# One large change to the gate, FFN and FFT-mixer training step: tail position, chain order, sigmoids, dB scaling and drain copies

## The chip, the cores and the metric

The kernel runs on one core of one Trainium2 chip. The metric is the device time of one execution in microseconds (us). Each of the kernel's executions is given, and their median is the kernel's time. A profiled execution also has a span (first to last recorded instruction) and a trace of every instruction.

## The reference

With S = 2048 tokens, D = 576 columns, F = 4608 hidden columns, all in bf16:

```python
g = sigmoid((x * gate_w).sum(-1, keepdims=True))
a = irfft2(rfft2(x) * (w_r + 1j * w_i))              # over tokens and columns
b = (gelu(x @ w_gate) * (x @ w_up)) @ w_down         # tanh form of gelu
out = g * a + (1 - g) * b
# returned: out, and for the given grad_out the gradients of
# x, w_r, w_i, w_gate, w_up, w_down, gate_w
```

The kernel names used below: dO is grad_out, dB = (1 - g) dO is the gradient that reaches b (held in SBUF, 128 tokens to a tile, 16 tiles), z = dO w_down^T, da = (1 - g) z, A the hidden activation gelu(gate)·up, dHg and dHu the gradients of the gate and up products. The gradient of w_down is A^T dB, those of w_gate and w_up are x^T dHg and x^T dHu.

## The kernel before

**Phase 1** loops over 18 column groups of F (g, FG = 256 columns each) and inside it over 4 token blocks (m, 4 tiles of 128 tokens). These 72 steps are numbered pr = 4 g + m from 0. A step does this:

- `H_mm` (lines 395 to 420) issues on TensorE: 16 full 128-row matmuls for z (line 402); whatever is handed in as `between`; the 4 row-tiled matmuls of z for the last 64 of the 576 contraction rows (line 407); and 4 row-tiled ones (64 rows) for xy, the gate and up products (line 411). `xy_full(0)` and `xy_full(1)` then issue the 8 + 8 full matmuls of xy (line 418). z has one PSUM buffer (its tag is shared with the transform's `pf`), xy has two.
- On ScalarE, `H_da` copies z into da, scaled, four instructions (line 430), and `H_act` evicts xy: q is the square of the gate product (line 437), xb the gate product (439), hu the up product (440).
- On VectorE, `H_ew1` (445 to 447) makes s, the argument of the tanh, and a polynomial in q. `H_ew2`, called `sigs()` in the loop, comes at the end of the step: ScalarE makes two sigmoids of s (lines 461, 462) and VectorE works a **chain** of eight operations (466 to 473) to A, dHu and dHg. A store (line 477, SP's queue) writes the three to DRAM for phase 2.
- da, xb and hu have two buffers each; q, s and om have one. dH comes from a ring (`keep`).

Between these stands other work for TensorE. **Weight-gradient units** of the group before (`W_units`) are split over the steps: `u_dwd` (line 509, 16 matmuls A·dB to a unit), `u_dw` (line 527, 16 matmuls x·dH), and one `tail` (line 541, 32 column-tiled matmuls for the last 64 columns of x). The tail is the `inside` job of step m = 2: it is handed to `H_mm` as `between`, so it lies between z's full and row-tiled matmuls, except in step 5, where it comes after `H_mm`. The units' PSUM results are copied out by `wevac` (line 486), on ScalarE, and on VectorE in step 6 after the point `run_late`. What is left of a group's units (`carry`, pend[4]) goes into the next group's first step. **Transform units** of the FFT branch (lines 570 to 850) are spread over the steps by a share of work, all through the one `pf` buffer, and evicted by ScalarE or VectorE. From about 370 to 630 us VectorE also has the products with w_r and w_i.

Group 0 is different: its steps 0 to 3 also transpose x and dO on TensorE (line 367) with copies on VectorE or ScalarE (line 374), compute the gate (line 383), and hold the chain back: the chain of step m runs in step m + 1 (`held`). Ahead of a held chain VectorE scales four tiles of dB in place (`scale_dB`, line 955), in steps 1 to 4. Step 5 builds two tables XR on VectorE (`build_R`, line 164); step 6 builds the B table (lines 225 to 239), whose last product (line 239) waits for a sine that ScalarE makes in `run_late`, between two loads of its function tables.

**Drain**: when the loop is over, the units of group 17 remain. The tail comes first, then `carry` (the last unit of group 16), then pend[0] to pend[4] (d0; d1 to d3; w0; w1 and w2; w3).

**Phase 2** (line 1168 on, matmuls of 128x288) makes b and the gradient of x from what was stored, fed by transposing loads (`pin`, six buffers, SP's queue).

## Time and profile before

| | us |
|---|---|
| median of 6 executions | 1413.31 |
| lowest, highest | 1412.71, 1415.09 |
| the profiled execution | 1414.85 |
| its span | 1413.1 |
| TensorE (PE) busy | 1378.0 |
| VectorE (DVE) busy | 734.1 |
| ScalarE (ACT) busy | 730.2 |
| GpSimd (POOL) busy | 244.6 |
| phase 2's first matmul (line 1168) at | 985.39 |
| mean granted TensorE clock | 0.996 |

How to read the views. A line of the timeline gives the start, the length and the engine of a run of equal instructions, the line of the kernel, the tile written and the tiles read with their shapes, the number of instructions, and in brackets how long the engine was idle before and who ended that ("<-DVE hu L472" is VectorE's instruction on line 472). A line of the windows gives a stretch, its length, the busy time and count of each engine (PE, the weight loads PEld, DVE, ACT, POOL), the granted TensorE clock (1.00 is full speed), the busy share of the DMA engines and GB/s. In the page's row PEclk each digit is the clock of a fortieth of the span in tenths, where 9 is 90% or more. Some matmul records are missing from the trace, so that a short idle time of PE with the releaser "issue" can be a lost record.

### The profile page before, as it was taken

The numbers are of one execution on the slowest core, as the hardware profiler recorded it, in microseconds if no ns is written. First come the engines' busy times: TensorE is split into PE (matmuls) and PEld (weight loads), VectorE is DVE, ScalarE is ACT, GpSimd is POOL, SyncE is SP. The second block draws the span as 40 slices with busy tenths as digits, with TensorE's granted clock in tenths as the row PEclk, the third lists the DMA queues.
The fourth block names the chain that finished last, engine by engine and source line by source line (L and its number), as shares of the span: only waits on it lengthen the run. The fifth ranks groups of instructions, "written<-read, shape, count | busy, mean of one in ns | idle before, by whom it ended". The sixth has DMA issues, their size and how long they took to land.

```text
span 1413.1 us, 25803 instructions
## 1 busy us (share of the span) xinstructions
PE 1378.0 (98%) x10181; PEld 915.1 (65%) x10272; DVE 734.1 (52%) x1400; ACT 730.2 (52%) x1325; POOL 244.6 (17%) x486
## 2 busy tenths in 40 slices
PE   8899999999999999999999999999999999999999
PEld 6456566565565556556566566555777777777777
DVE  7866565655788777885565656551000642212101
ACT  6777776777787878777777776671000000000000
POOL 3010101113353633423101111110000100000000
PEclk9999999999999999999999999999999999999999
DMA  6334344445455665556456464759999998777773
GB/s 206 101 87 133 94 135 120 108 118 164 119 132 152 159 164 147 134 150 164 127 142 169 128 170 134 182 122 263 191 187 202 223 193 166 166 158 163 158 151 90
DMA packets 510645, 214.48 MB, mean 152 GB/s; under 512 B 312538, under 2 KB 503708, under 8 KB 510524
## 3 DMA queue, kind: packets, MB, share of 16 engines
q1 hardware_dynamic: 493402, 187.44, 56.8%
q0 software_dynamic: 14912, 24.24, 6.1%
q8 instruction: 80, 1.31, 0.4%
q10 hardware_dynamic: 2210, 1.15, 0.3%
q14 instruction: 41, 0.34, 0.1%
HBM read 41.05 MB, written 93.84 MB: 95 GB/s over the span
## 4 chain that ended last, share of the span: by engine, by line
PE 87%; ACT 4%; issue 1%; DVE 1%; DVEq 0%
PE acc L1168 30%; PE wps L527 15%; PE xy L418 15%; PE wps L509 9%; PE z L402 8%; PE wps L541 2%; PE xy L411 2%; PE pf L570 2%; PE z L407 1%; PE pf L841 1%; ACT xb L439 1%; ACT q L437 1%; PE pf L768 1%; PE pf L843 1%; ACT hu L440 1%
## 5 line engine op out<-in xcount | busy, mean ns | idle before, releaser
L1168 PEld LDWEIGHTS <-pin 128*128 128x128 bf16 x3456 | 338.0, 98 | 85.8 <-issue 0.3
L527 PE MATMUL wps<-dH,xn 128*128 128x512 bf16 x1122 | 270.3, 381 | 4.4 <-DVE dwd L486 2.6
L418 PE MATMUL xy<-wgu,xT 128*128 128x512 bf16 x1091 | 259.8, 381 | 8.4 <-issue 7.6
L418 PEld LDWEIGHTS <-xT 128*128 128x128 bf16 x1152 | 106.9, 98 | 138.1 <-issue 31.0
L527 PEld LDWEIGHTS <-xn 128*128 128x128 bf16 x1152 | 111.8, 98 | 122.1 <-issue 5.8
L1185 ACT COPY bo<-acc 128x288 f32<-128x288 f32 x32 | 12.7, 398 | 305.0 <-PE acc L1168 280.4
L466 DVE TENSOR_TENSOR xb<-xb,s 128x1024 bf16<-128x1024 bf16 x72 | 49.8, 692 | 203.4 <-ACT s L462 203.3
L509 PE MATMUL wps<-dB,A 128*128 128x288 bf16 x1152 | 153.6, 286 | 0.0
L534 POOL DMA_DIRECT2D out_dram<-dw x134 | 72.8, 546 | 458.1 <-ACT dw L486 432.4
L1168 PE MATMUL acc<-wgT,pin 128*128 128x288 bf16 x1152 | 143.8, 286 | 0.0
L1168 PE MATMUL acc<-wuT,pin 128*128 128x288 bf16 x1152 | 143.6, 286 | 0.0
L1168 PE MATMUL acc<-wd_all,pin 128*128 128x288 bf16 x1152 | 142.6, 286 | 0.0
L402 PE MATMUL z<-wdT,dOT 128*128 128x256 bf16 x1152 | 138.1, 273 | 2.9 <-ACT Xg L684 1.0
L509 PEld LDWEIGHTS <-A 128*128 128x128 bf16 x1152 | 112.2, 98 | 33.1
L402 PEld LDWEIGHTS <-dOT 128*128 128x128 bf16 x1152 | 112.8, 98 | 26.7 <-issue 6.3
L430 ACT ACTIVATE da<-z,omg 128x256 bf16<-128x256 f32 x288 | 112.0, 470 | 9.0 <-PE z L407 4.9
L1240 DVE SCALAR_TENSOR_TENSOR f32t<-gwf,dlog,b16t 128x576 f32<-128x576 f32 x16 | 13.1, 818 | 175.5 <-DMA b16t<-dxa_scr 175.5
L439 ACT CAST xb<-xy 128x512 bf16<-128x512 f32 x144 | 85.1, 591 | 31.3 <-PE xy L418 31.3
L437 ACT ACTIVATE q<-xy 128x512 bf16<-128x512 f32 x144 | 88.1, 613 | 7.4 <-PE xy L418 5.3
L440 ACT CAST hu<-xy 128x512 bf16<-128x512 f32 x144 | 87.4, 607 | 0.0
L461 ACT ACTIVATE om<-s 128x1024 bf16<-128x1024 bf16 x72 | 76.3, 1060 | 5.8 <-DVE s L446 5.8
L486 ACT CAST dw<-wps 128x512 bf16<-128x512 f32 x72 | 42.1, 586 | 70.4 <-PE wps L527 66.8
(207 smaller groups left out, 1585.0 us busy)
## 6 DMA issues: line engine op xcount, KB each, us to landing
scr<-dH SPq DMA_DIRECT2D x144, 256.0 KB, 3.4
scr<-A SPq DMA_DIRECT2D x72, 256.0 KB, 2.5
out_dram<-dw POOLq DMA_DIRECT2D x134, 64.0 KB, 2.3
wd_all<-in_B_w_down_dram SPq DMA_DIRECT2D x3, 1728.0 KB, 8.2
out_dram<-dwd POOLq DMA_DIRECT2D x34, 144.0 KB, 3.3
scr_p<-Vt SPq DMA_DIRECT2D x32, 145.0 KB, 2.8
wgu<-in_B_w_gate_dram SPq DMA_DIRECT2D x18, 256.0 KB, 3.9
wgu<-in_B_w_up_dram SPq DMA_DIRECT2D x18, 256.0 KB, 3.4
```

Source lines behind the costliest of these rows:

```text
L402: nc.tensor.matmul(zo(t), lhsT=dOT[:, ci, t, :], rhs=wdT[:, ci, :], start=(t % 4 < 2 and ci == 0), stop=False)
L418: nc.tensor.matmul(xy[k][:, t % 2, :], lhsT=xT[:, ci, t, :], rhs=wgu[:, ci, :], start=False, stop=(ci == 3))
L430: nc.scalar.activation(da[:, t, :], z[:, t % 2, t // 2, :], ACT.Copy, scale=omg32[:, 4 * m + t:4 * m + t + 1])
L437: nc.scalar.activation(q[:, h, :], xy[:, :, 0:FG], ACT.Square)
L439: nc.scalar.copy(xb[:, h, :], xy[:, :, 0:FG])
L440: nc.scalar.copy(hu[:, h, :], xy[:, :, FG:2 * FG])
L461: nc.scalar.activation(om[:], s[:], ACT.Sigmoid, scale=-2.0 * C_GELU)
L466: V.tensor_tensor(xb[:], xb[:], s[:], op=ALU.mult)
L509: nc.tensor.matmul(wps[:, :288], lhsT=tl(0, t)[:, fch * P:(fch + 1) * P], rhs=dB[:, t, h * 288:(h + 1) * 288], start=(t == 0), stop=(t == ...
L527: nc.tensor.matmul(wps[:].rearrange("p a b -> p (a b)"), lhsT=xn[:, t, c * P:(c + 1) * P], rhs=kt[t // 4][1][:, t % 4].rearrange("p k f -> ...
L534: wst[0].dma_start(ov[:, c, fsl], dw[:, k, :])
L1168: nc.tensor.matmul(acc[:, :288], lhsT=src[:, r, :], rhs=w_of(r)[:, h * 288:(h + 1) * 288], start=(first and r == 0), stop=(last and r == F ...
```

## The change

Eight edits:

1. The `inside` job (the tail) comes after `H_mm` and `H_da` in every step, so between the row-tiled matmuls of xy and `xy_full(0)`.
2. dH is taken from its ring in `H_ew1`, where da·hu is written into dHg; in the chain dHu = da·xb comes second. The chain's last product is then made in place in dHg.
3. In groups 0 and 1 and in every step m = 2 only one sigmoid is made; 1 - s is made on VectorE into xb's buffer. In the other steps both sigmoids are made, the one that the chain needs first; the tag `om` becomes `sg`.
4. dB is scaled in steps 4 (tiles 0 to 3, ScalarE), 5 (4 to 7 ScalarE, 8 to 11 VectorE) and 6 (12 to 15, VectorE). Group 0's weight units are ordered anew: w2 in step 5, all four dwd units in step 6, w3 later.
5. The first copy of a transposed x tile goes to ScalarE in steps 1 and 2.
6. `build_R` for later tables adds a constant to the table before it, in place of four multiply-adds.
7. The B table's last product is issued after the step's other jobs and stores.
8. In the drain `carry` and d0 to d3 come ahead of the tail, and the copies of the dw results use the buffers of xb, hu and da in turn. The stores are ordered A, dHu, dHg.

```diff
--- before.py
+++ after.py
@@ -160,8 +160,15 @@
     n = 4
     step = 2.0 * math.pi / S * EPS_SCALE
     X = unit([n, P], I32, name="XR")
-    for t in range(n):
-        V.scalar_tensor_tensor(X[:, t, :], tb.kk[:, 0, :], tb.scol[:, t0 + t:t0 + t + 1], tb.kk[:, 1, :], op0=ALU.mult, op1=ALU.add)
+    if t0 == 0:
+        for t in range(n):
+            V.scalar_tensor_tensor(X[:, t, :], tb.kk[:, 0, :], tb.scol[:, t0 + t:t0 + t + 1], tb.kk[:, 1, :], op0=ALU.mult, op1=ALU.add)
+    else:
+        if t0 == n:
+            tb.k4 = unit([P], I32, name="k4")
+            V.tensor_scalar(tb.k4[:], tb.kk[:, 0, :], float(n), None, op0=ALU.mult)
+        V.tensor_tensor(X[:], tb.XR[:], tb.k4[:].unsqueeze(1).to_broadcast([P, n, P]), op=ALU.add)
+    tb.XR = X
     V.tensor_single_scalar(X[:], X[:], S - 1, op=ALU.bitwise_and)
     if t0 % 8 == 0:
         tb.Rpair = unit([8, P], name="Rt")
@@ -236,8 +243,12 @@
 
     def sines():
         nc.scalar.activation(o[:], Xi[:].rearrange("p v a b c d -> p v (a b c d)"), ACT.Sin, bias=tb.pi[:], scale=-step)
+
+    def signed():
         V.tensor_tensor(tb.B[:], o[:], ms[:].rearrange("p v a b c d -> p v (a b c d)"), op=ALU.mult)
     tb.late.append(sines)
+    yield
+    signed()
     yield
 
 
@@ -420,7 +431,7 @@
         return z, full
 
     def ewt(tag, g):
-        if tag in ("q", "s", "om"):
+        if tag in ("q", "s", "sg"):
             return unit([4, FG], name=tag) if g == 0 else ew.tile([P, 4, FG], BF16, tag=tag, name=tag, bufs=1)
         return ew.tile([P, 4, FG], BF16, tag=tag, name=tag, bufs=2)
 
@@ -439,13 +450,15 @@
             nc.scalar.copy(xb[:, h, :], xy[:, :, 0:FG])
             nc.scalar.copy(hu[:, h, :], xy[:, :, FG:2 * FG])
 
-    def H_ew1(g, tiles):
+    def H_ew1(g, tiles, da):
         xb, q, hu = tiles
         s = ewt("s", g)
         V.tensor_scalar(s[:], q[:], A_GELU, 1.0, op0=ALU.mult, op1=ALU.add)
         V.tensor_tensor(s[:], xb[:], s[:], op=ALU.mult)
         V.tensor_scalar(q[:], q[:], 6.0 * A_GELU * C_GELU, 2.0 * C_GELU, op0=ALU.mult, op1=ALU.add)
-        return s
+        dH = keep.tile([P, 4, 2, FG], BF16, tag="dH", name="dH")
+        V.tensor_tensor(dH[:, :, 0, :], da[:], hu[:], op=ALU.mult)
+        return s, dH
 
     stores = []
 
@@ -455,25 +468,30 @@
             stores.pop(0)()
             n -= 1
 
-    def H_ew2(g, m, tiles, s, da):
+    def H_ew2(g, m, tiles, s, dH, da):
         xb, q, hu = tiles
-        om = ewt("om", g)
-        nc.scalar.activation(om[:], s[:], ACT.Sigmoid, scale=-2.0 * C_GELU)
-        nc.scalar.activation(s[:], s[:], ACT.Sigmoid, scale=2.0 * C_GELU)
+        one = g < 2 or m == 2
+        if one:
+            om = xb
+            nc.scalar.activation(s[:], s[:], ACT.Sigmoid, scale=2.0 * C_GELU)
+        else:
+            om, s = s, ewt("sg", g)
+            nc.scalar.activation(s[:], om[:], ACT.Sigmoid, scale=2.0 * C_GELU)
+            nc.scalar.activation(om[:], om[:], ACT.Sigmoid, scale=-2.0 * C_GELU)
         A = keepA.tile([P, 4, FG], BF16, tag="A", name="A")
-        dH = keep.tile([P, 4, 2, FG], BF16, tag="dH", name="dH")
         dHg, dHu = dH[:, :, 0, :], dH[:, :, 1, :]
         V.tensor_tensor(xb[:], xb[:], s[:], op=ALU.mult)
+        V.tensor_tensor(dHu, da[:], xb[:], op=ALU.mult)
+        V.tensor_tensor(A[:], xb[:], hu[:], op=ALU.mult)
         V.tensor_tensor(q[:], xb[:], q[:], op=ALU.mult)
+        if one:
+            V.tensor_scalar(om[:], s[:], -1.0, 1.0, op0=ALU.mult, op1=ALU.add)
         V.tensor_tensor(om[:], om[:], q[:], op=ALU.mult)
-        V.tensor_tensor(A[:], xb[:], hu[:], op=ALU.mult)
-        V.tensor_tensor(dHu, da[:], xb[:], op=ALU.mult)
         V.tensor_tensor(om[:], om[:], s[:], op=ALU.add)
-        V.tensor_tensor(hu[:], da[:], hu[:], op=ALU.mult)
-        V.tensor_tensor(dHg, hu[:], om[:], op=ALU.mult)
+        V.tensor_tensor(dHg, dHg, om[:], op=ALU.mult)
         fsl = slice(g * FG, (g + 1) * FG)
         def store():
-            for k, tl in enumerate((A[:], dHg, dHu)):
+            for k, tl in ((0, A[:]), (2, dHu), (1, dHg)):
                 LD.dma_start(scr[k][m][:, :, fsl].rearrange("t p f -> p t f"), tl)
         stores.append(store)
         kept.setdefault(g, []).append((A, dH))
@@ -484,6 +502,14 @@
 
     def wevac(out, in_):
         wcopy[0](out, in_)
+
+    spare = []
+
+    def dwtile(name):
+        if not spare:
+            return stage.tile([P, 2, FG], BF16, tag="dw", name=name)
+        spare.append(spare.pop(0))
+        return ew.tile([P, 4, FG], BF16, tag=spare[-1], name=name, bufs=2)[:, 0:2, :]
 
     def W_units(g):
         fsl = slice(g * FG, (g + 1) * FG)
@@ -528,7 +554,7 @@
                                      rhs=kt[t // 4][1][:, t % 4].rearrange("p k f -> p (k f)"), start=(t == 0), stop=(t == T - 1))
                 if t1 < T:
                     return
-                dw = stage.tile([P, 2, FG], BF16, tag="dw", name="dw")
+                dw = dwtile("dw")
                 wevac(dw[:], wps[:])
                 for k, ov in enumerate((o4v, o5v)):
                     wst[0].dma_start(ov[:, c, fsl], dw[:, k, :])
@@ -540,14 +566,14 @@
                 for k, r in ((1, LO), (2, HI)):
                     nc.tensor.matmul(wps[r, 0, :], lhsT=xn[:, t, 512:576], rhs=tl(k, t),
                                      start=(t == 0), stop=(t == T - 1))
-            dw = stage.tile([P, TPB, FG], BF16, tag="dw", name="dwt")
+            dw = dwtile("dwt")
             wevac(dw[:, 0], wps[:, 0, :])
             wst[0].dma_start(out_4[512:576, fsl], dw[LO, 0, :])
             wst[0].dma_start(out_5[512:576, fsl], dw[HI, 0, :])
         w = [u_dw(c, (0, 12, T)) if g == 0 and c < 2 else u_dw(c) for c in range(4)]
         d = [u_dwd(fch, h) for fch in range(FCH) for h in range(2)]
         if g == 0:
-            return [[w[0][:1], w[1][:1]], [d[0], d[1]], [d[2], d[3], w[2][:2]], [w[2][2:], w[3][:2]], w[3][2:], {1: [w[0][1][1], w[1][1][1]], 2: [tail]}]
+            return [[w[0][:1], w[1][:1]], [w[2]], [d[0], d[1], d[2], d[3]], [w[3][:3]], w[3][3:], {1: [w[0][1][1], w[1][1][1]], 2: [tail]}]
         return [[d[0]], [d[1], d[2], d[3]], [w[0]], [w[1], w[2]], w[3], {2: [tail]}]
 
 
@@ -950,9 +976,12 @@
 
     carry, pend, held, rest = [], None, [], []
 
-    def scale_dB(k):
+    def scale_dB(k, cp):
         for t in range(4 * k, 4 * k + 4):
-            V.tensor_scalar(dB[:, t, :], dB[:, t, :], omg32[:, t:t + 1], None, op0=ALU.mult)
+            if cp == AC:
+                nc.scalar.activation(dB[:, t, :], dB[:, t, :], ACT.Copy, scale=omg32[:, t:t + 1])
+            else:
+                V.tensor_scalar(dB[:, t, :], dB[:, t, :], omg32[:, t:t + 1], None, op0=ALU.mult)
 
     for g in range(NG):
         if g == 1:
@@ -973,13 +1002,13 @@
             state = []
 
             def sigs(g=g, m=m, tiles=tiles, state=state):
-                H_ew2(g, m, tiles, state[0], state[1])
+                H_ew2(g, m, tiles, *state)
             if g == 0:
                 def items(src, dst, t, *cp):
                     return titems(src, dst, 4 * t, (pgtile,) * 3, cp) if t < NPR else [None] * 3
                 do1 = items(dB, dOT, 1, VC, VC, VC) if m == 0 else []
                 do2 = items(dB, dOT, m + 2, AC, AC, VC)
-                x1 = items(xn, xT, m + 1, VC, VC, VC)
+                x1 = items(xn, xT, m + 1, AC if m else VC, VC, VC)
                 z, xy_full = H_mm(g, m, ([opening] if m == 0 else []) + rest)
                 rest = []
                 da = H_da(g, m, z)
@@ -995,7 +1024,6 @@
                 for f in mid_:
                     f()
                 if held:
-                    scale_dB(m - 1)
                     held.pop()()
                 for part in (1, 0):
                     H_act(0, xy, tiles, part)
@@ -1020,18 +1048,16 @@
                     do2[0]()
                     do2[1]()
                     rest = [do2[2]]
-                state += [H_ew1(g, tiles), da]
+                state += [*H_ew1(g, tiles, da), da]
                 held.append(sigs)
             else:
-                split = pr == 5
-                z, xy_full = H_mm(g, m, [] if split else inside)
+                z, xy_full = H_mm(g, m)
                 da = H_da(g, m, z)
-                if split:
-                    for f in inside:
-                        f()
+                for f in inside:
+                    f()
                 xy = xy_full(0)
                 if held:
-                    scale_dB(NPR - 1)
+                    scale_dB(0, AC)
                     held.pop()()
                 for part in (1, 0):
                     H_act(0, xy, tiles, part)
@@ -1039,11 +1065,14 @@
                 xy = xy_full(1, fft_next if k0 else None)
                 for part in range(2):
                     H_act(1, xy, tiles, part)
-                state += [H_ew1(g, tiles), da]
+                state += [*H_ew1(g, tiles, da), da]
                 if pr == 5:
+                    scale_dB(1, AC)
+                    scale_dB(2, VC)
                     build_R(nc, tb, unit, 8)
                     build_R(nc, tb, unit, 12)
                 elif pr == 6:
+                    scale_dB(3, VC)
                     next(makeB)
                 side_work(4.4)
                 jobs = carry + hs
@@ -1066,6 +1095,8 @@
                     fft_next()
                     k += 1
                 flush()
+                if pr == 6:
+                    next(makeB)
                 if pr < NG * NPR - 1:
                     sigs()
             carry = []
@@ -1114,9 +1145,12 @@
     for f0 in range(0, NFC, FCB):
         LD.dma_start(wd_all[:, f0:f0 + FCB, :], wd_v[:, f0:f0 + FCB, :])
     wst[0] = nc.scalar
+    spare += ["xb", "hu", "da"]
+    for _, h in carry + [h for us in pend[:2] for u in us for h in u]:
+        h()
     for f in pend[5][2]:
         f()
-    for _, h in carry + [h for us in pend[:4] for u in us for h in u] + pend[4]:
+    for _, h in [h for us in pend[2:4] for u in us for h in u] + pend[4]:
         h()
     ps1.close()
     wstack.close()
```

## The prediction

> **What bounds the kernel now.** I read the page's busy shares and slices first, then the windows with the granted clock, the table of PE's waits, and the timeline around each of its long waits.
>
> ```profile
> PE 1378.0 (98%) x10181; PEld 915.1 (65%) x10272; DVE 734.1 (52%) x1400; ACT 730.2 (52%) x1325; POOL 244.6 (17%) x486
> ...
> PEclk9999999999999999999999999999999999999999
> ```
>
> TensorE sets the time: 1378.0 of 1413.1 us busy. Only its 35.1 us of holes and its slow matmuls are there to win; much of the holes is matmul records missing from the trace (1091 of 1152 on line 418). VectorE and ScalarE are about half idle, so their work counts only where PE waits for it. The change removes no matmul. The windows tell which holes cost twice:
>
> ```profile
> 50.00:60.00 10.00, 7.68 (x28) 3.08 (x29) 8.97 (x19) 7.68 (x16) 0.00 (x0) 0.83 0.27 80
> ...
> 90.00:100.00 10.00, 9.59 (x49) 4.88 (x50) 5.84 (x10) 6.04 (x10) 0.58 (x1) 0.83 0.05 16
> 950.00:960.00 10.00, 7.56 (x54) 4.09 (x54) 6.17 (x10) 3.54 (x5) 2.14 (x4) 0.90 0.43 131
> ```
>
> The number ahead of the last two is the granted clock. It leaves 1.00 in these three places (and on in 960 to 970, 0.93); each follows the longest waits of PE: step 4 (1.23 + 1.06 us), step 6 (2.63) and the drain (2.25). By single microseconds it is 0.50 for about 3 us behind each. The lone wait of 1.28 at 37.0 left it at 1.00. So a wait of over 2 us, or two near each other, costs itself and some 1.6 us of slow matmuls.
>
> **Start, steps 3 and 4.**
>
> ```profile
> 51.15 0.39 PE L411 MATMUL xy<-wgu,xT 64*128 64x512 bf16 x2 [1.23 <-ACT q L437]
> 52.60 0.39 PE L411 MATMUL xy<-wgu,xT 64*128 64x512 bf16 x2 [1.06 <-ACT hu L440]
> 52.93 5.31 PE L418 MATMUL xy<-wgu,xT 128*128 128x512 bf16 x15
> ```
> ```profile
> 45.72 1.57 ACT L430 ACTIVATE da<-z,omg 128x256 bf16<-128x256 f32 x4 [2.29 <-DVE hu L472]
> ```
>
> PE waits for ScalarE's evictions, and these are late because da waited 2.29 us for the seventh operation of an older chain (line 472), the last reader of its buffer. The change reads da for the last time in the chain's second operation, so this wait goes: z is ready at 43.3, da can start there. ScalarE also loses one sigmoid (1.06 us). The evictions come 2.7 us sooner (2.29 + 1.08, less 0.7 that the sigmoid then waits for s on VectorE). A second count agrees roughly: PE's waits fall from 1.23 + 1.06 to about 0.55, and the dOT copy that PE awaits at 37.0 comes 0.55 earlier, since an xT copy goes to ScalarE and four dB scalings (4 x 0.30) leave VectorE: 1.74 + 0.55 = 2.3. I take 2.5. With one wait of 0.55 the clock should hold: sixteen matmuls of line 418 took 5.15 us here (52.93 to 58.08) and take 3.40 at 44.45: 1.75. **Gain 4.2**; 2.3 if the clock dips still.
>
> The dB scaling that replaces VectorE's is put on ScalarE in steps 4 and 5 (4 activations of 128x576 each). No row has it: from 0.59 (a copy of 512 from PSUM) to 0.74 each (580 elements, line 577); I take 0.65, 2.6 a group. In step 4 the evictions then still end about 3 us before the row-tiled matmuls need their buffer; were that cover gone, up to 2.6. I count 0. Step 5's VectorE group (1.2) lies in 1.9 us that VectorE waits there anyway.
>
> **Steps 6 and 7.**
>
> ```profile
> 89.51 0.42 DVE L239 TENSOR_TENSOR Btab<-oB,msB 128x256 bf16<-128x256 f32 x1 [2.33 <-ACT oB L238]
> 89.86 0.82 DVE L486 CAST dwd<-wps 128x288 bf16<-128x288 f32 x2
> ```
> ```profile
> 90.36 2.96 PE L527 MATMUL wps<-dH,xn 128*128 128x512 bf16 x7 [2.63 <-DVE dwd L486]
> ```
>
> Two dwd copies stood 2.33 us on VectorE's queue behind the B table's product, which waits for ScalarE's sines (two table loads and 3.05 us of sines). The change puts that product behind the step's copies: the 2.63 and about 1.6 of slow clock go, 4.2. Instead, the dB of tiles 12 to 15 is scaled on VectorE only in this step, behind the first three operations on s and q and the new da*hu, and the four dwd units (all now in this step) read it: the first stops until each tile is ready, about 1.2 + 3 x 0.2, less some overlap 1.7; the third waits 0.35 for its copy behind the table's ten small operations. In step 7 fewer weight-gradient matmuls stand between transform units and one wait of about 0.3 is new. 4.2 - 1.7 - 0.35 - 0.3 = **1.9**. If the broken stall still trips the clock, 0.2; if the scaling is hidden wholly, 3. The changed XR tables use an integer add that no row has: between 0.69 (a product of 1024 in bf16) and 1.14 (the four operations it replaces); below what it replaces, off PE's path: 0.
>
> **Drain.**
>
> ```profile
> 954.45 1.50 PE L541 MATMUL wps<-dH,xn 128*64 128x256 bf16 x24
> 958.20 1.06 PE L541 MATMUL wps<-dH,xn 128*64 128x256 bf16 x8 [2.25 <-DVE dH L473]
> ```
>
> The tail needs the last chain's dH (ended 958.15). The change first issues 16 matmuls of carry (3.45) and 64 of line 509 (8.0): these need only A, which is ready by 953.7 in the new order (955.6 before), and the tail comes at about 966, dHg ready at 956.6. So 2.25 of wait and the slow matmuls behind it (line 527 spaced at 0.427 instead of 0.215 from 959.2 to 961.3, and the eight of line 541 at half clock) go: 2.25 + 1.55 = **3.8**. Phase 2 follows at once; its transposed loads are issued when the stores are done and PE has waited on none of them (its waits on loads there sum to under 0.3), so its 427.7 us should stay. The six spare tiles for copies remove a wait of ScalarE (3.06 at 975.2) on which PE didn't wait: 0.
>
> **Every step: the chain and q.** The chain takes 5.2 us now (206.13 to 211.32). With two sigmoids it becomes seven operations, 4.7; with one (groups 0 and 1, and every step 2 of four) eight with the 0.42 us 1 - s, 5.1. As the needed sigmoid is now first or alone, the chain starts 1.08 sooner where it waits for it (203 us of waits in 66 steps). But q has one buffer, and its last reader moves from third to fifth or sixth:
>
> ```profile
> 206.13 0.69 DVE L466 TENSOR_TENSOR xb<-xb,s 128x1024 bf16<-128x1024 bf16 x1 [5.21 <-ACT s L462]
> ...
> 207.58 0.69 DVE L468 TENSOR_TENSOR om<-om,q 128x1024 bf16<-128x1024 bf16 x1
> ```
> ```profile
> 208.89 0.62 ACT L437 ACTIVATE q<-xy 128x512 bf16<-128x512 f32 x1
> ```
>
> Margin here 208.89 - 208.27 = 0.62. The reader's end moves from +2.13 to +3.36 (two) or +3.77 (one) behind a start 1.08 earlier: 0.15 or 0.56 later, inside the margin (0.48 to 0.85 in most steps; 2.5 in the tail's). But in about six steps between 370 and 630 VectorE is busy, and the chain starts late whatever the sigmoid:
>
> ```profile
> 474.44 0.68 DVE L466 TENSOR_TENSOR xb<-xb,s 128x1024 bf16<-128x1024 bf16 x1
> ...
> 475.88 0.69 DVE L468 TENSOR_TENSOR om<-om,q 128x1024 bf16<-128x1024 bf16 x1
> ```
>
> There q's eviction (at 477.14) must wait to about 478.8: 1.7; by the same count 0.9, 1.2, 2.2 and 2.2 in the others, 0.35 in one. PE sees it only through the single buffer of the transform units: some 0.85 at 480.5 (line 679) and 0.9 at 583.3; in the others its next such matmul comes later than the delayed copy. **Loss 1.7**, bounds 0 and 6.
>
> **The tail's place.** It now stands behind the row-tiled matmuls in 17 steps: as many changes of tile shape, but row to column is in no row. The shown ones cost 0.09 to 0.16 us (0.16 idle ahead of line 418), so -0.1 to +0.1 a step: 0, both ends 1.5. da leaves sooner, but ScalarE idles 0.25 to 0.7 before xb anyway. dH taken earlier from its ring waits for a unit that ran just before: 0. The stores on SP's queue are as many and none of PE's waits is for a load of weights: 0.
>
> **Sum.** -4.2 - 1.9 - 3.8 + 1.7 = -8.2. From the profiled execution (1414.85, span 1413.1 and 1.75 around it) 1406.6; that one lies 1.5 above the median shown, so from the median 1413.31: **1405.1**.
>
> **A rule against this.** The granted clock fell after waits of 2.63 and 2.25 us. The Trainium skill ("TensorE: Matmul & The Clock Gate", Part 1, "What's actually happening") has the clock fall after an idle window of about 3.4 us. Taken strictly, none of these waits should have cost clock, and by it the gain would be 4.9 less (-3.3); the rows decide.
>
> **Rivals.**
> - *The clock dips anyway* in step 4 or 6 (new broken waits of 1 to 2 us): a loss of 1.75 or 1.7, both 3.5: 1407 to 1408.6. Against it: 1.28 alone did nothing. Chance 0.13.
> - *More is won*: q costs PE nothing, switches are no dearer: -9.9, with cheaper switches -11.4: 1402 to 1403.4. Chance 0.15.
> - *q stalls spread* in VectorE's busy stretch (3 to 6 instead of 1.7): 1406.4 to 1409.4. Chance 0.10.
> - *Slower*: the single q. If chains don't start sooner in ordinary steps (s late on VectorE through the new da*hu, 0.6), q is freed 1.2 to 1.6 later against margins of 0.5 to 0.85: ScalarE loses 0.5 to 0.8 in each of about 50 steps, and with 0.25 reaching PE in 72 steps that is 18 us: -9.9 + 18, 1421. It decides from 0.14 us a step (9.9 / 72). Against it: the 5 us for which the chain waits on the sigmoid alone. Chance 0.05.
>
> The forecast has 0.57. Its own terms at their ends give 1399.6 to 1411; range 1399.5 to 1411. About 0.2% (2.8 us) is what a measurement of this kernel can tell from no change. Faster by more: the first four cases less their upper ends, 0.92; within, 0.03; slower, 0.05.
>
> **What would show it.** Right: no clock under 1.00 in 50 to 60 and behind the drain's first matmuls; no 2.29 wait of da; PE's line 541 no longer waiting for dH; phase 2 starting near 977 and lasting 427.7. Wrong: PE waiting in step 6 on VectorE's dB for over 2 us; ScalarE's q waiting on VectorE in ordinary steps; new holes at the tail.

## The result and the profile after

The changed kernel takes 1409.32 us (median of 16 executions, 1408.86 to 1409.67) against 1413.17 (36 executions, 1411.66 to 1415.17): 3.85 us less, ratio 0.9973 with an interval of [0.9966, 0.9979]. The forecast was 8.2 us less. Its profiled execution took 1409.1, span 1407.2, 5.75 us less than the profiled one of before (1414.85). So two things call for an answer: why the two profiles differ by 5.75 and not 8.2, and why the medians differ by only 3.85.

The page of after has TensorE as the bound as before, and the rows of windows have the clock at 1.00 in every stretch that was lowered before:

```profile
PE 1375.2 (98%) x10182; PEld 913.9 (65%) x10272; DVE 748.8 (53%) x1408; ACT 712.4 (51%) x1309; POOL 245.3 (17%) x486
```
```profile
50.00:60.00 10.00, 9.88 (x50) 4.90 (x51) 9.24 (x18) 7.99 (x16) 0.00 (x0) 1.00 0.44 133
...
90.00:100.00 10.00, 9.25 (x56) 4.72 (x55) 7.42 (x14) 6.54 (x13) 0.05 (x1) 1.00 0.06 20
...
956.00:966.00 10.00, 9.95 (x97) 7.85 (x97) 0.21 (x2) 2.43 (x6) 0.00 (x0) 1.00 1.18 234
```

A ledger says more than the sums. Every step begins with the same 16 full matmuls for z; the table has the start of these in after less that in before (the profiled executions), in us, and beside it three experiments, told below.

| start of | before, at | after | q_early | da_early | before_again |
|---|---|---|---|---|---|
| step 0 | 8.10 | +0.23 | +0.16 | -0.06 | -0.02 |
| step 4 | 47.69 | -0.31 | -0.39 | +0.01 | +1.58 |
| step 5 | 63.26 | -4.22 | -4.30 | -2.29 | -0.11 |
| step 9 | 118.32 | -5.17 | -5.25 | -3.96 | -0.27 |
| step 29 | 394.79 | -5.16 | -5.23 | -3.94 | -0.26 |
| step 30 | 407.51 | -4.66 | -5.22 | -3.94 | -0.25 |
| step 34 | 458.84 | -4.11 | -5.22 | -3.93 | -0.25 |
| step 36 | 485.36 | -3.01 | -5.23 | -3.93 | -0.25 |
| step 44 | 588.13 | -2.13 | -5.22 | -3.92 | -0.25 |
| step 71 | 941.39 | -2.13 | -5.22 | -3.75 | -0.24 |
| phase 2 | 985.39 | -6.09 | -9.16 | -6.46 | -1.75 |

So after wins 4.45 from step 0 to step 5, 0.95 in steps 5 to 8, loses 3.04 in four steps between 29 and 44, and wins 3.96 in the drain. Between these places the steps keep time to 0.02 us, those with the moved tail too. (Within steps 5 to 8 work was moved from step to step, so only their sum says something.)

The start. The timeline of PE in step 4, and of ScalarE's da, of after:

```profile
50.07 0.39 PE L422 MATMUL xy<-wgu,xT 64*128 64x512 bf16 x2 [0.24 <-ACT hu L451]
50.40 3.63 PE L429 MATMUL xy<-wgu,xT 128*128 128x512 bf16 x15
```
```profile
43.64 1.57 ACT L441 ACTIVATE da<-z,omg 128x256 bf16<-128x256 f32 x4 [0.52 <-PE z L418]
46.05 1.06 ACT L476 ACTIVATE s<-s 128x1024 bf16<-128x1024 bf16 x1 [0.84 <-DVE s L457]
```

The two waits of 1.23 and 1.06 are one of 0.24, da waits for PE and for no buffer, and fifteen records of line 429 take 3.63, where those of line 418 took 5.31.

Steps 6 to 8, PE's timeline of after:

```profile
81.54 7.17 PE L535 MATMUL wps<-dB,A 128*128 128x288 bf16 x52 [0.95 <-DVE dB L984]
...
101.03 1.91 PE L413 MATMUL z<-wdT,dOT 128*128 128x256 bf16 x16 [0.78 <-ACT ve L616]
...
110.19 0.91 PE L596 MATMUL pf<-Dt,xT 128*128 128x290 bf16 x6 [1.06 <-ACT ve L616]
```

The wait of 2.63 is gone. In its place stand 0.95 for dB, some 0.7 within the 52 matmuls behind it (64 of them took 8.00 in the drain, so 52 should take 6.5), and 0.78 and 1.06 for evictions of transform units.

The middle. In before, ScalarE's eviction of q in steps 35 and 43 followed without a wait:

```profile
477.14 0.62 ACT L437 ACTIVATE q<-xy 128x512 bf16<-128x512 f32 x1
...
579.91 0.62 ACT L437 ACTIVATE q<-xy 128x512 bf16<-128x512 f32 x1
```

ScalarE's timeline of after in the windows of steps 33, 35 and 43, and one of the waits that PE then had in step 35:

```profile
447.97 0.60 ACT L448 ACTIVATE q<-xy 128x512 bf16<-128x512 f32 x1 [0.87 <-DVE s L489]
...
474.82 0.60 ACT L448 ACTIVATE q<-xy 128x512 bf16<-128x512 f32 x1 [1.68 <-DVE xb L489]
...
579.22 0.60 ACT L448 ACTIVATE q<-xy 128x512 bf16<-128x512 f32 x1 [2.20 <-DVE xb L489]
```
```profile
479.52 0.41 PE L705 MATMUL pf<-Vp,Btab 128*128 128x289 bf16 x2 [0.63 <-ACT Xg L710]
```

Line 489 is the chain's om*q, the last reader of q's one buffer.

The drain, PE's timeline of after: the tail follows without a wait.

```profile
955.68 8.00 PE L535 MATMUL wps<-dB,A 128*128 128x288 bf16 x64
963.61 1.94 PE L567 MATMUL wps<-dH,xn 128*64 128x256 bf16 x32
```

### The profile page after: what moved, and what is told of

Read it like the earlier page. It is cut to its first block, busy times and chain, and to the rows that moved or that the text cites. A ratio compares the mean times of both kernels' runs of the same rounds, so it can differ in the third digit from the quotient of the medians.

```text
span 1407.2 us, 25935 instructions
## 1 busy us (share of the span) xinstructions
PE 1375.2 (98%) x10182; PEld 913.9 (65%) x10272; DVE 748.8 (53%) x1408; ACT 712.4 (51%) x1309; POOL 245.3 (17%) x486
## 3 DMA queue, kind: packets, MB, share of 16 engines
q10 hardware_dynamic: 2210, 1.15, 0.3%
## 4 chain that ended last, share of the span: by engine, by line
PE 55%; ACT 1%; DMA 1%; SPq 1%; DVE 1%; issue 1%; ACTq 0%
PE acc L1202 30%; PE wps L553 7%; PE xy L429 7%; PE wps L535 4%; PE z L413 4%; PE wps L567 1%; DMA wd_all<-in_B_w_down_dram 1%; PE xy L422 1%; SPq L1127 1%; PE z L418 1%; PE pf L867 1%; PE pf L869 1%; ACT ZT L844 0%; PE pf L841 0%; ACT hu L451 0%
## 5 line engine op out<-in xcount | busy, mean ns | idle before, releaser
L483 DVE TENSOR_TENSOR xb<-xb,sg 128x1024 bf16<-128x1024 bf16 x48 | 33.2, 692 | 104.1 <-ACT sg L479 104.1
L1233 DVE SCALAR_TENSOR_TENSOR b16t<-b16t,g,f32t 128x576 bf16<-128x576 bf16 x16 | 13.1, 818 | 95.4 <-DMA b16t<-a_scr 95.1
```

Source lines behind the costliest of these rows:

```text
L483: V.tensor_tensor(xb[:], xb[:], s[:], op=ALU.mult)
```

## The experiments

All medians are in us. The last column has the median of before that was taken beside the run (21 to 23 executions, 36 for after).

| kernel | median | executions | before beside it |
|---|---|---|---|
| before_again | 1413.27 | 11 | 1413.11 |
| after | 1409.32 | 16 | 1413.17 |
| q_early | 1406.94 | 5 | 1413.11 |
| pool_dB (on q_early) | 1406.57 | 5 | 1413.35 |
| pool_dB5 (on q_early) | 1407.98 | 5 | 1413.25 |
| w3_half (on after) | 1409.30 | 7 | 1413.35 |
| old_drain (on after) | 1409.46 | 7 | 1413.25 |
| dB_early (on after) | 1412.04 | 11 | 1413.25 |
| d3_later (on after) | 1413.52 | 11 | 1413.11 |
| da_early (on before) | 1410.74 | 11 | 1413.35 |
| sig_first (on before) | 1411.60 | 11 | 1412.26 |
| da_sig (on before) | 1411.88 | 11 | 1412.26 |
| drain_full (on before) | 1412.31 | 11 | 1413.35 |
| drain_wd (on before) | 1416.07 | 11 | 1413.25 |
| drain_only (on before) | 1417.79 | 5 | 1413.11 |

### before_again: do executions of one kernel differ in their clock?

No edit.

> The kernel before, unchanged, to see the granted clock and span of many executions side by side. Theory 1 (the clock's dips differ from execution to execution): three dips of about 1.6 us each were in the profiled execution (clock 0.996, 1414.85 us), and others have one or two: the times fall in groups near 1411.8, 1413.2 and 1414.9, and the mean clock rises as the time falls, by about 0.0012 for each 1.6 us. Rival: every execution has the same three dips, and the spread comes from loads or from what lies around the span: the clock is 0.996 in all of them, whatever the time.

Measured: theory 1. Of 98 executions of before with a mean clock each, 29 took 1411.6 to 1412.3 (clock 0.999, one 0.998), 51 took 1412.8 to 1413.4 (0.997 or 0.998), and 18 took 1414.8 to 1415.2 (0.996); there is nothing between (of the 36 executions of the result, which have no clock beside them, one lies between, at 1413.80). The profiled one of this run (1413.11, clock 0.997) has these windows, over the start, step 4, step 6 and the drain; the clock is the number ahead of the last two:

```profile
15.00:20.00 5.00, 5.00 (x31) 2.82 (x31) 3.06 (x8) 2.97 (x9) 0.00 (x0) 0.67 1.06 340
53.00:57.00 4.00, 2.94 (x16) 1.28 (x14) 3.93 (x9) 2.23 (x7) 0.00 (x0) 1.00 0.24 69
90.00:94.00 4.00, 3.75 (x13) 1.62 (x13) 1.67 (x4) 2.78 (x3) 0.57 (x1) 0.58 0.11 37
957.00:962.00 5.00, 4.04 (x25) 1.95 (x25) 0.88 (x2) 0.37 (x1) 0.00 (x0) 1.00 0.72 193
```

It dips at 15 to 20 and in step 6, and in neither of the two others, though the same waits are there: PE's timeline of this run has the drain's wait, and the matmuls behind it at full clock (0.63, where the profile of before had 1.06):

```profile
957.96 0.63 PE L541 MATMUL wps<-dH,xn 128*64 128x256 bf16 x8 [2.25 <-DVE dH L473]
```

The profile that I had worked from was of an execution with three dips, the slowest group; the median execution has two. Each costs 1.5 to 1.75.

The traces also show what decides. In all 16 profiles every full stretch of half clock lasts 3.41 us, and within an execution the stretches start whole multiples of 3.41 us apart (in before at 53.47, 91.02 and 958.00: 11 and 254 of them). So the clock seems to be set anew every 3.41 us, by what PE did in the 3.41 us before. Windows laid on this grid show it. In before, these are the three just ahead of its dips, and, second, the first dip itself:

```profile
50.06:53.47 3.41, 1.26 (x7) 0.50 (x7) 3.34 (x6) 2.49 (x6) 0.00 (x0) 1.00 0.02 6
53.47:56.88 3.41, 3.41 (x9) 1.21 (x9) 3.24 (x9) 2.04 (x5) 0.00 (x0) 0.50 0.54 156
87.61:91.02 3.41, 0.73 (x4) 0.30 (x4) 1.16 (x3) 3.38 (x6) 0.05 (x1) 1.00 0.13 37
954.59:958.00 3.41, 1.36 (x24) 1.20 (x22) 3.38 (x6) 0.56 (x1) 1.35 (x3) 1.00 0.49 154
```

In the three, PE (the first busy time) was idle for 2.15, 2.68 and 2.05 us. In before_again the grid lies elsewhere, and its lines cut the same waits of step 4 and of the drain in two:

```profile
48.99:52.40 3.41, 2.52 (x23) 1.78 (x21) 2.62 (x8) 3.30 (x5) 0.00 (x0) 1.00 0.48 143
52.40:55.81 3.41, 2.02 (x10) 0.79 (x10) 3.37 (x6) 1.73 (x4) 0.00 (x0) 1.00 0.26 76
953.53:956.94 3.41, 2.19 (x28) 1.48 (x27) 3.38 (x6) 0.59 (x1) 1.99 (x4) 1.00 0.28 91
956.94:960.35 3.41, 2.39 (x17) 1.24 (x17) 0.94 (x2) 0.37 (x1) 0.00 (x0) 1.00 0.64 188
```

No window holds more than 1.4 us of idle there, and no dip followed. From 20 us on, in the 16 profiles, all eleven windows with 2.05 us or more of idle were followed by a dip, and none with 1.75 or less was; between, 1.86 was (sig_first) and 2.02 was not (da_early). The dips at 15 us, in four of the profiles, came after 1.2 us of idle among the small matmuls of the start and do not fit this count; they stay open.

### q_early: is the middle's loss q?

```diff
...                                # left out: group 0 keeps the order of after; om is tile "sg" in the others
+        else:
+            if one:
+                V.tensor_scalar(om[:], s[:], -1.0, 1.0, op0=ALU.mult, op1=ALU.add)
+            V.tensor_tensor(q[:], xb[:], q[:], op=ALU.mult)
+            V.tensor_tensor(om[:], om[:], q[:], op=ALU.mult)
+            V.tensor_tensor(dHu, da[:], xb[:], op=ALU.mult)
+            V.tensor_tensor(A[:], xb[:], hu[:], op=ALU.mult)
```

> After, with the operation that reads q last put third in the chain (fourth with one sigmoid, for which the spare tile sg takes 1 - s) in all groups but the first; the same instructions otherwise. Theory 2 (q's single buffer, held longer, costs the 3.0 us that steps 29 to 44 lose against before): ScalarE's waits of 0.87, 1.68 and 2.20 us ahead of q go, the steps keep their lead of about 5.2 us, and the median falls by 2.5 to 3.1 us to about 1406.5. Rival (VectorE's added work, da*hu in front of the chain, makes everything behind it late): the waits move elsewhere and under 1 us comes back.

Measured: 1406.94, 2.4 under after, just short of the 2.5 to 3.1 expected. The ledger keeps its 5.2 from step 9 to step 71, so all of the 3.04 came back; 0.5 of it was lost again in phase 2 of the profiled execution (428.4 against 427.9). ScalarE's timeline in the windows of steps 35 and 43 (line 494 is om*q here):

```profile
472.25 0.60 ACT L448 ACTIVATE q<-xy 128x512 bf16<-128x512 f32 x1 [0.23 <-DVE sg L494]
...
575.64 0.60 ACT L448 ACTIVATE q<-xy 128x512 bf16<-128x512 f32 x1 [0.83 <-DVE sg L494]
```

Of 1.68 and 2.20, 0.23 and 0.83 are left, too little to reach PE. The rival (VectorE is merely fuller) falls: the instructions are the same, in another order.

### drain_only, drain_full, drain_wd, old_drain: what is the drain's edit worth?

drain_only has the reordering alone on before. drain_full adds the spare tiles. drain_wd also moves the loads of w_down:

```diff
-        LD.dma_start(wd_all[:, f0:f0 + FCB, :], wd_v[:, f0:f0 + FCB, :])   # ahead of the drain
...
+        nc.scalar.dma_start(wd_all[:, f0:f0 + FCB, :], wd_v[:, f0:f0 + FCB, :])   # behind it
```

old_drain is after with the drain of before.

> Before, with the new order of the drain alone (carry and the four dwd units ahead of the tail; the copies keep their two tiles). Theory 1: the wait of 2.25 us always goes, the slow matmuls behind it (1.55 us) only in executions that had them: phase 2 starts 2.2 to 3.9 us sooner in a profile, and the median is 2.3 to 3.0 us under that of before, not 3.8. Rival (the step was sized right in the forecast): 3.8 us in the median. Second rival (phase 2 is fed by loads and gives it back): under 1 us.

> Before, with the whole of the drain's edit: the new order of the units and the copies of dw results in the six tiles of xb, hu and da. The order alone had phase 2 begin 3.95 us sooner after the last step, and then lost 6.9 us because its second pair of accumulators waited 5.25 us for a copy that had waited for a store to leave its tile. If the six tiles are what mends this: the start of phase 2 as there, no wait of over 1 us for a copy, and 2.3 to 3.5 us less than before in the median. If the stores themselves are late (they share the DMA engines with 5 MB of weights loaded at the same time): the copies get their tiles, and 2 us or more of wait stay.

> Before with the whole drain edit, and the three loads of w_down (wd_all, 5 MB) issued on ScalarE's queue behind the last copy, not on SP's queue ahead of the drain. With the loads at 972 to 975, two stores of dw took 7.6 us to issue, the next copy waited 8.2 us and phase 2's second pair of accumulators 2.7 us. If the loads crowd out the stores: those waits go, the issue takes about 0.85, phase 2 takes 427.7 us, and the median falls 2 to 2.8 us below the drain edit's 1412.3. If the stores are slow for another reason (their 512-byte rows, the transposing loads): nothing changes; and if the loads then come too late, PE waits for wd_all near 1008.

> After, with edit 8's order and spare tiles undone: the tail first, the copies in two tiles. The step lead of about 2.1 us at the last step stays; what the drain is worth inside the changed kernel is read from the medians. If it is worth what the wait and the slow matmuls came to in the profiled execution of before: 3.8 us slower than after, 1413.1. If only the wait (2.25 us) and the half clock of some executions: 2.3 to 3.0 slower, 1411.6 to 1412.3. If it is as little as the edit alone brought to before (1.0 us): 1410.3.

Measured, from the last step's start to phase 2's first matmul, and from there to the end of the span:

| profile | drain | phase 2 |
|---|---|---|
| before (dip), before_again (none) | 44.00, 42.49 | 427.7, 427.7 |
| drain_only | 40.05 | 434.5 |
| drain_full | 40.05 | 430.5 |
| drain_wd | 40.05 | 434.3 |
| after | 40.04 | 427.9 |
| old_drain | 40.05 | 429.2 |

The order does take the wait away on before, as forecast, but phase 2 gives it back, with 6.9 us in drain_only (a wait of 5.25, and a dip behind it at 987.55), so that the kernel was 4.7 us slower, where all three expectations had it faster. With the spare tiles (drain_full) it was 1.0 faster than the before beside it, where 2.3 to 3.5 was expected if the tiles were the cure. PE's and ScalarE's timelines of drain_only ("ACTq" is an issue of a transfer on ScalarE's queue):

```profile
988.00 7.23 PE L1170 MATMUL acc<-wgT,pin 128*128 128x288 bf16 x46 [5.25 <-ACT dw L486]
```
```profile
975.32 7.10 ACTq L534 DMA_DIRECT2D out_dram<-dw  x2
982.53 0.59 ACT L486 CAST dw<-wps 128x512 bf16<-128x512 f32 x1 [7.54 <-DMA wd_all<-in_B_w_down_dram]
983.15 0.85 ACTq L534 DMA_DIRECT2D out_dram<-dw  x2
987.37 0.59 ACT L486 CAST dw<-wps 128x512 bf16<-128x512 f32 x1 [4.25 <-DMA out_dram<-dw]
```

Two stores of dw took 7.1 us to issue on ScalarE, beside the loads of w_down, while ScalarE's next copy stood behind them; the last copy then waited 4.25 us for a store to leave one of two tiles, and phase 2's second pair of accumulators for that copy. Six tiles take away the second wait (PE still waits 2.69 in drain_full). With the loads behind the copies (drain_wd) the stores issue in 0.82 each and PE waits for no copy, which agrees with the loads crowding them out. They don't always: in before the loads were issued from 972.5 to 978.8, and two stores at 975.85 took 1.03; in after two took 3.66. What sets the amount stays open. In drain_wd PE then waits 4.9 us in seven places for phase 2's own inputs (`pin`), probably because the loads now run beside those, so it is worse still. Its timeline:

```profile
1009.27 20.91 PE L1179 MATMUL acc<-wd_all,pin 128*128 128x288 bf16 x166 [1.37 <-DMA pin<-scr]
```

old_drain is the surprise: 1409.46, the same as after within the scatter (1409.00 to 1410.60), nearest to the lowest of its three expectations and below even that. PE's timeline of it shows why:

```profile
952.63 1.94 PE L567 MATMUL wps<-dH,xn 128*64 128x256 bf16 x32
...
982.45 7.51 PE L1199 MATMUL acc<-wgT,pin 128*128 128x288 bf16 x60 [1.20 <-ACT dw L504]
```

The tail, first again, has all 32 matmuls at once: dH is there already. So the drain got shorter by other edits than the drain's. What edit 8 adds is that the 1.20 at the hand-over goes, in that execution; in the medians it is worth 0.1 (that execution is the slowest of old_drain's seven).

### da_early, sig_first, da_sig: which edits shortened the drain, and what did da's buffer cost?

da_early is edit 2 alone on before, sig_first has only the two sigmoids exchanged, da_sig both:

```diff
-        nc.scalar.activation(om[:], s[:], ACT.Sigmoid, scale=-2.0 * C_GELU)
-        nc.scalar.activation(s[:], s[:], ACT.Sigmoid, scale=2.0 * C_GELU)
+        om, s = s, ewt("om", g)
+        nc.scalar.activation(s[:], om[:], ACT.Sigmoid, scale=2.0 * C_GELU)
+        nc.scalar.activation(om[:], om[:], ACT.Sigmoid, scale=-2.0 * C_GELU)
```

> Before, with edit 2 alone: da*hu goes into dH ahead of the chain, da*xb is the chain's second operation, om*q its fourth; two sigmoids in the old order, dB and copies as before. If da's wait for its buffer is what makes steps 3 and 4 slow: the 2.29 us of wait ahead of da go, PE's two waits on line 411 shrink to under 0.7 together, and step 5 starts 1.7 to 2.4 us sooner than in executions of before without a dip in step 4. Steps 29 to 44 lose 0.5 to 1.5 us, since q is free 0.7 us later. Net 0.5 to 2 us less in the median. Rival (the sigmoid and the scalings on VectorE are as much of it): less than 1 us at step 5.

> Before, with the two sigmoids of each step in the other order: the one that the chain's first operation needs is made first, the other in the place of its argument. Nothing else. If the drain's wait falls by what the chain starts sooner: 2.25 - 1.08 = 1.2 us of wait stay at line 541, the drain takes 41.4 us against 42.49 without a dip. q is free 1.08 sooner, so the steps from 29 to 44 don't lose. Median 1 to 2.5 us under before, since a shorter wait trips the clock less often. If the drain's wait hangs on the length of the chain alone: no change there.

> Before, with edit 2 (da*hu ahead of the chain) and the sigmoids in the other order; the drain, the dB scaling and the tail as before. Together the two take 1.2 (edit 2) and 1.1 (order) from the drain's wait: no wait at line 541, the drain at 40.05 us with the old order of its units, so that edit 8 has nothing left to remove. Median 1409.3 to 1410.3. If the order of the drain's units were needed after all, 0.5 us or more of wait would stay there.

Measured: the tail's wait for dH, 2.25 in before, is 1.05 in da_early, 0.42 in sig_first and none in da_sig, whose drain takes 40.05 with the old order. That settles it: the chain ends sooner (one product less in it, and its first sigmoid first), and that is the drain's gain. sig_first took 1.83 and not 1.08: its last chain began 1.9 us sooner after the step's start. The medians missed. da_sig was expected at 1409.3 to 1410.3 and came at 1411.88: in its profile phase 2 lost 2.58 at the same copy as in drain_full, and the scatter from 1410.35 to 1414.82 is probably that hand-over too. sig_first is only 0.66 under the before beside it, where 1 to 2.5 was expected: a difference that its scatter doesn't tell from none.

At the start da_early fell short of its mechanism. da no longer waits for its buffer, but ScalarE's next instruction then waits for VectorE, as its timeline shows:

```profile
46.90 1.06 ACT L463 ACTIVATE om<-s 128x1024 bf16<-128x1024 bf16 x1 [1.37 <-DVE s L446]
```

Evictions came 0.6 sooner, not 2.3, and PE's two waits were still 0.62 and 1.06. That step 5 began 2.29 sooner is 0.54 of wait, so the rival (under 1 us) was right, and 1.75 of a dip that this execution didn't have. The 0.5 to 1.5 expected to be lost in steps 29 to 44 was 0.2. It also went through step 6's wait of 2.63 without a dip, and steps 5 to 8 took 1.67 less than in before: the price of a dip there. Its median, 2.6 under before and more than the 0.5 to 2 expected, goes with a clock of 0.998 to 1.000: its tail's shorter wait and fewer dips.

### dB_early: what did moving the dB scaling bring the start?

```diff
                 if held:
+                    scale_dB(m - 1, VC)
                     held.pop()()
...                                          # left out; below, step 4. The scalings of steps 5 and 6 go
-                    scale_dB(0, AC)
+                    scale_dB(NPR - 1, VC)
                     held.pop()()
```

> After, with edit 4's scaling undone: VectorE scales dB ahead of each held chain in steps 1 to 4, as before; the order of the units stays. The scaling is 4 x 0.30 us in front of the chains that decide steps 3 and 4: if it is what the start gained beside da's wait and the sigmoid, PE's waits on line 422 in step 4 come back to 1.0 to 1.5 us together and step 5 starts 0.8 to 1.5 us later than in after; step 6 loses no time for dB and wins 0.95 to 1.7: the sum within 0.7 us of after. If the late scaling did nothing at the start, step 5 is as in after and the median 1 to 1.7 us better.

Measured: step 5 starts 2.13 later than in after, more than expected, and steps 5 to 8 win 0.84 more. The median is 2.7 slower than after's, not within 0.7 of it. In PE's timeline the wait at 37 us, 0.75 in after, is 1.85, and one of step 4's two is back; ScalarE's shows the reason, since its sigmoid waits 1.95 for s on VectorE, 0.84 in after:

```profile
37.72 0.61 PE L378 MATMUL pf<-ident,xn 128*128 128x128 bf16 x8 [1.85 <-DVE dOT L385]
...
52.20 0.39 PE L422 MATMUL xy<-wgu,xT 64*128 64x512 bf16 x2 [1.06 <-ACT hu L451]
```
```profile
48.18 1.06 ACT L476 ACTIVATE s<-s 128x1024 bf16<-128x1024 bf16 x1 [1.95 <-DVE s L457]
```

So without the scaling's move about 2 of the start's 2.7 us (4.45 less the dip) are lost again: VectorE's queue held the evictions, and da's buffer only stood in front of it. No run has the scaling's move, the single sigmoid or the moved xT copy alone on before, so what each would bring by itself is not shown. Its executions also form two groups, 1410.4 to 1410.9 at clock 1.000 and 1412.0 to 1412.6 at 0.999: a dip is 1.6 us in a kernel's times too.

### w3_half, d3_later, pool_dB, pool_dB5: steps 6 to 8

The edits in short:

```diff
-            ... [d[0], d[1], d[2], d[3]], [w[3][:3]], w[3][3:], ...
+            ... [d[0], d[1], d[2], d[3]], [w[3][:2]], w[3][2:], ...          # w3_half
+            ... [d[0], d[1], d[2]], [d[3], w[3][:2]], w[3][2:], ...          # d3_later
+  nc.gpsimd.tensor_scalar(dB[:, t, :], dB[:, t, :], omg32[:, t:t + 1], ...)  # pool_dB: tiles 12 to 15, step 4; pool_dB5: step 5
```

> After, with w3 of group 0 cut in halves: 8 matmuls in step 7 and 8 in step 8, in place of 12 and 4. If a wait of the transform's unit is set by how much other work stands beside it: the 1.06 us in step 8 falls to 0.2, and the waits of step 7 (0.59 and 0.78) grow by about 0.9 together: under 0.3 us in the sum. If the wait in step 8 is a matter of its own, 0.8 us less.

> After, with the fourth dwd unit of group 0 in step 7 instead of step 6, and w3 halved between steps 7 and 8 (8 and 8 matmuls, not 12 and 4). Theory 3 (steps 6 to 8 gave back 3.6 us: 0.95 and some 0.8 for the late dB, and 0.78 + 1.06 because too few weight matmuls stand between the transform's units to hide its evictions): the waits of 0.78 ahead of step 8 and of 1.06 inside it go, 1.5 to 1.9 us, median near 1407.6. Rival (those waits are the transform's own chain and stay whatever stands between): under 0.5 us.

> The version with q read early, and the scaling of dB's tiles 12 to 15 on GpSimd in step 4, not on VectorE in step 6. If the dB that comes late costs 0.95 us and the 0.8 in pieces behind it in step 6: both go, median 1405.2 (1.7 less than the version it starts from). If GpSimd's instructions slow VectorE's beside them, or push the stores of weight gradients that GpSimd issues, PE waits anew in steps 4 to 6 and less than 0.5 comes.

> As the GpSimd version, with its four scalings issued in step 5 instead of step 4. In step 4 they took 8.7 us, and VectorE's products beside them 1.12 to 1.15 instead of 0.69, which made PE wait 0.93 for an eviction and ate the 0.95 won in step 6. If that is all of it: step 5 starts where the version with q early has it (4.3 us ahead of before), step 7 another 0.9 to 1.7 sooner, median 1405.2 to 1406. If GpSimd slows VectorE's copies and products in steps 5 and 6 as well: under 0.4 better than 1406.9.

w3_half: as the first expectation had it. The wait in step 8 fell from 1.06 to 0.22, and one of 0.77 appeared in step 7; the median is after's. So in this run the waits for transform evictions kept their sum, and only their place followed the weight matmuls.

d3_later was a miss, 4.2 slower than after. VectorE's and PE's timelines:

```profile
94.22 0.69 DVE L485 TENSOR_TENSOR A<-xb,hu 128x1024 bf16<-128x1024 bf16 x1 [5.18 <-PE wps L535]
```
```profile
99.45 0.64 PE L613 MATMUL pf<-Y,Rt 128*128 128x290 bf16 x2 [4.78 <-ACT Y L601]
```

A has a ring of six tiles, and group 0's are read by d3. With d3 in step 7, the chain of step 6 stops at its third product until PE has read them, with q's last reader behind it; so q's eviction waits on VectorE, Y's behind it on ScalarE, and PE for Y. The order of the units in the change is held by that ring.

pool_dB took the 0.95 out of step 6, but step 4 gave it up: step 5 began 0.7 later than in q_early, both counted from step 0. GpSimd took 8.71 us for the four tiles, and VectorE's products beside it took 1.12 and 1.15 where they take 0.69 (its timeline):

```profile
43.62 1.12 DVE L497 TENSOR_TENSOR xb<-xb,s 128x1024 bf16<-128x1024 bf16 x1
...
48.10 1.15 DVE L483 TENSOR_TENSOR xb<-xb,s 128x1024 bf16<-128x1024 bf16 x1
```

pool_dB5 is 1.0 slower than q_early, which neither expectation had. Its scalings ran from 67.0 to 75.9, behind GpSimd's stores; VectorE's own dB scaling beside them took 2.51 instead of 1.20, the chain of step 5 ended late, and the copies of dwd with it (PE's timeline):

```profile
85.39 4.08 PE L542 MATMUL wps<-dB,A 128*128 128x288 bf16 x32 [2.63 <-DVE dwd L511]
```

The 1406.57 of pool_dB and the 1406.94 of q_early can't be told apart with five executions each. Both beat before and after.

## Why the forecast missed by half

Point by point, in the prediction's own terms:

- **"So a wait of over 2 us, or two near each other, costs itself and some 1.6 us of slow matmuls"** is the first failed step. The price is right (1.5 to 1.75), the "so" is not: the same waits were followed by a dip in one execution and not in another, as the idle time fell into one window of 3.41 us or into two. The working then took a difference that held three dips from a profile and set it against the median, whose execution has two. That is 1.7 us of the miss (1414.85 against 1413.17); after's profiled execution lies 0.2 under its own median. The text had seen that its profile lay 1.5 above the median, and explained nothing by it.
- **Start, 4.2:** measured 4.45, of which 1.75 was the dip. The size was right, the cause half: dB_early puts about 2.0 on VectorE's dB scaling, da_early 0.5 on da's buffer, which the text had as the chief cause.
- **Steps 6 and 7, 1.9:** measured 0.95. The step that failed is "one wait of about 0.3 is new": it was 0.78 in step 7 and 1.06 in step 8, which the working didn't look at. dB's 1.7 and the copy's 0.35 came to 1.65 together (0.95 and 0.7).
- **Drain, 3.8:** measured 3.96, and for a wrong reason. The working credited the new order with a wait that the chain's edits had taken (da_sig, old_drain). It even has the number, dHg ready 1.55 sooner at 956.6, and did not ask what the old order would do with that. Without the dip it is 2.45. That the six tiles "remove a wait of ScalarE (3.06 at 975.2) on which PE didn't wait: 0" failed too: with the new order and two tiles, that wait reached PE (drain_only).
- **q, loss 1.7:** the mechanism and ScalarE's waits were right (1.68 and 2.20 against 1.7 and 2.2); their price for PE was 3.04. Steps 29 and 33 were counted at nothing and lost 0.50 and 0.55; step 35 lost 1.11, where 0.85 was counted; step 43 lost 0.88 (0.9).
- **The tail's place, 0:** right: the steps with it keep time to 0.02.
- The rest is small: the first loads 0.23 later, phase 2 0.24, outside the span 0.1.
- The range, 1399.6 to 1411, is not what the terms give at their stated ends: these sum to 1400.8 (4.2, 3, 3.8 and 1.5 won, q free) and 1414.5 (2.3, 0.2 and 3.8 won, 6 and 1.5 lost).

Together, the 8.2 gains 0.25 at the start and 0.15 in the drain and loses 0.95 in steps 5 to 8, 1.35 by q and 0.55 by small things, which is the 5.75 of the profiles; the 1.7 and 0.2 by which the two profiles lie beside their medians leave 3.85.

Without any dip in either, the profiles differ by 5.75 - 4.9 (1.75, 1.67 as da_early has it, and 1.5) = 0.85 us. By the ledger, the waits that the change takes away are worth 7.8 (2.7 at the start, 2.63 in step 6, 2.45 in the drain), and what it adds is about 7.0 (3.35 in steps 5 to 8, 3.04 in the middle, 0.55 of small things). So of the 3.85 in the medians, about 0.85 is waits and the other 3 the two dips that no longer happen: after's mean clock is 1.000 in all its executions. That last division is worked out from the profiles and the groups of times; no run holds the clock alone fixed. And one of the dips is perhaps not the change's doing: the one at 15 us, which before_again has, lies where no edit took a long wait away, and w3_half, the same kernel up to step 6, has it in its profile. That none of after's 17 executions has it is not explained.

The rivals: "the clock dips anyway" was wrong, and the slower case (q in every step) did not occur. "q stalls spread" (3 to 6 us, 1406.4 to 1409.4) came in by its size, 3.04; that 1409.32 lies in its range as well is luck, since it has the error of the dips in it. "More is won" (1402 to 1403.4) did not come: even q_early, in which q costs nothing, stands at 1406.94.

## What to carry to other kernels

Before you take a difference from a profile, put the profiled execution among the other times of its kernel: where these fall in groups, find out what differs between them, and take gains from the group that the median is in. When several edits each explain the same wait, count it once, and ask for each what is left when the others are made. And a chain that frees a single buffer late is paid where its engine is already full, so put the last reader of a scarce buffer first among operations that are free to move.

## What the runs showed of the hardware

- The TensorE clock halves for 3.41 us at a time, on a grid of 3.41 us whose place differs between executions. From 20 us on it followed every window with 2.05 us or more of PE idle (eleven in 16 profiles) and none with 1.75 or less; so the same wait of 2.25 or 2.63 us is followed by it in one execution and not in another. It also fell at 15 us in some, after 1.2 us of idle. The Trainium skill ("TensorE: Matmul & The Clock Gate", Part 1, "What's actually happening") tells of a window that is free-running and of about 3.4 us, which agrees with the 3.41. That a whole window must be idle, as the prediction took its rule, does not agree: 2.05 us sufficed. The -3.3 that the prediction worked out from this rule lies nearer to the measured -3.85 than its own sum, but not for the rule's reason, since the dips were there.
- GpSimd's four scalings of 128x576 took 8.7 to 9.0 us, and VectorE's 0.69 us products took up to 1.15 beside them, its 0.30 us scalings 0.63. The skill ("GPSIMD Engine Reference", section 8, "Key points") says that the two share their SBUF interfaces, which agrees.
- An issue of two transfers on ScalarE's queue took 0.82 to 0.86 us in quiet. Beside 5 MB of loads it took anything from 1.03 us (before) over 3.66 (after) to 7.10 and 7.62 (drain_only, drain_full), and held up ScalarE's own copies for that long.
